# Layer-norm statistics shared between VectorE and ScalarE, and one group of small matmuls moved, in a two-layer spectral and MLP kernel

## The chip, the cores and the metric

The kernel runs on one core of one Trainium2 chip. The metric is the device time of one execution in microseconds (us), median of several. Every time below comes from runs that were classed as undisturbed ("fast"). One profile is one execution.

## The reference, cut to what matters

```python
x = A_x                                              # 2048 x 1024, bf16
x = x + A(layernorm(x), w_r, w_i)                    # 2D FFT, filter, inverse FFT
x = x + B(layernorm(x), w1, b1, w2)                  # mish MLP, 1024 -> 3584 -> 1024
x = x + A(layernorm(x), w_r, w_i)
x = x + B(layernorm(x), w1, b1, w2)

def layernorm(x, eps=1e-5):
    m = jnp.mean(x, axis=-1, keepdims=True)
    v = jnp.var(x, axis=-1, keepdims=True)
    return (x - m) / jnp.sqrt(v + eps)
```

The change touches the very first layernorm, over sixteen tiles of 128 rows, and the point where each A hands over to its B.

## The kernel before

The first layernorm is not applied to x. Its scales 1/std are multiplied into the table of the first FFT stage ("scaled"), so the first matmul has to wait for the scales of all sixteen tiles. The statistics are made by two engines, each taking whole tiles:

```python
def first_scales(self):
    for j in range(10):
        self.stats_dve(j)              # VectorE: two bn_stats of 512, one bn_aggr
    for j in range(10, 16):
        self.stats_act(j)              # ScalarE: Copy and Square, each with accum_out
    self.sums_to_mv(10, 6)             # the combining step, VectorE
    self.root(0, 16)                   # sqrt on ScalarE, reciprocal on VectorE
    ...                                # transpose the scales: RT (SBUF) and a copy in PSUM

def scaled(self, j):                   # table of column group j times the scales
    if j == 3: ...                     # ScalarE, 8 small ones
    prog = self.pool if j in (1, 4, 6, 8, 10, 12, 14, 15) else self.dve
    self.op(prog, lambda e: e.tensor_tensor(self.MN.ap[:, n, :], ..., ALU.mult), ...)
```

GpSimd (`pool`) has a second duty before that. It issues twelve of the loads of x in its second layout, and holds them back until the last tile of the first layout has landed:

```python
for q in range(4):
    for h in range(8):
        prog = self.pool if q and h % 2 else sp
        self.dma(prog, self.XR.ap[h:P:8, 32 * q:32 * q + 32, :], ...,
                 reads=[self.r_xs[15]] if prog is self.pool else [])
```

At the start of layer B, `rest(bank)` is a group of fifteen matmuls of 96 columns that finishes a piece of A, and copies the result out on ScalarE. `transposed` transposes a normalised tile on TensorE and copies it out on VectorE. `mm1` is the first MLP matmul:

```python
self.root(0, 2)
rest(0)
for j in range(2):
    xn[j] = self.apply(j)
for j in range(2):
    transposed(0, j, xn[j])
self.warm(ACT.Mish)                    # loads the Mish table
rest(3)
...
for fg in range(4):
    mm1(0, fg, 0, ...)
    rest(3)
```

## Time and profile before

| | us |
|---|---|
| time, median of the first three runs | 1014.7 (1014.44 to 1017.05) |
| statistics: combining step starts | 20.12 |
| scales ready | 22.52 |
| GpSimd's table scalings start | 23.28 |
| first matmul of the second FFT stage (L719) | 40.07 |
| layer B of layer 0: first small group (L1014, 96 columns) | 119.89 |
| first large matmul (L1103) | 124.12 |

The numbers (but for the first row) are starts in the profiled execution, counted from the start of the span; for the scales it is the end of the copy that brings them in place. Each row is a place where one engine waits for another. The profile names instructions by source line; the changed kernel has seven lines more, so its line numbers are up to 7 higher, and its L441 is the new sum where L441 before is ScalarE's pass.

### The profile page before, as it was taken

What the parts mean: (1) busy time and instruction counts of PE and PEld (TensorE: products, weight loads), DVE (VectorE), ACT (ScalarE), POOL (GpSimd) and SP (SyncE); (2) the same over time, 40 slices, a digit from 0 to 9 for tenths busy, and PEclk for the clock granted to TensorE, in tenths of its full rate; (3) what the DMA queues carried; (4) which work ended last, traced back from release to release, by engine and by line L of the source; (5) the groups of instructions that cost most, each with busy time, mean ns of one, the idle gap of its engine ahead of it and who ended that gap; (6) DMA issues with size and microseconds to landing.
All of it is one profiled execution on the core that took longest, in us unless ns stands there. A gap on an engine that the chain in (4) does not pass through costs nothing.

```text
span 1013.4 us, 13752 instructions
## 1 busy us (share of the span) xinstructions
PE 958.2 (95%) x5826; PEld 506.4 (50%) x5826; DVE 326.5 (32%) x679; ACT 347.7 (34%) x487; POOL 81.5 (8%) x114
## 2 busy tenths in 40 slices
PE   0799799999999999999999979999999999999998
PEld 0667575444444444444456748644444444444443
DVE  6797568002444000033347736830011100000111
ACT  7798474440000443300029837534100023430000
POOL 3831000000000000002421100000000000000000
PEclk9999899999999999999999998999999999999999
DMA  9969823652111220002922875246411212100000
GB/s 281 281 191 321 213 60 115 198 196 65 48 46 32 74 82 21 1 21 85 199 60 84 232 187 154 77 161 203 129 25 45 73 52 83 43 1 11 21 27 26
DMA packets 154205, 107.00 MB, mean 106 GB/s; under 512 B 74448, under 2 KB 133664, under 8 KB 154144
## 3 DMA queue, kind: packets, MB, share of 16 engines
q1 hardware_dynamic: 143056, 78.61, 27.5%
q0 software_dynamic: 8912, 25.84, 8.7%
q10 hardware_dynamic: 2176, 1.66, 0.5%
q8 instruction: 47, 0.77, 0.3%
q14 instruction: 14, 0.11, 0.0%
HBM read 80.85 MB, written 20.71 MB: 100 GB/s over the span
## 4 chain that ended last, share of the span: by engine, by line
PE 87%; DVE 5%; DMA 4%; ACT 2%; POOL 1%; issue 0%; SPq 0%; ACTq 0%; POOLq 0%; DVEq 0%
PE PS L1121 38%; PE PS L1103 38%; PE PS L793 2%; PE PS L719 2%; PE PS L1014 2%; PE PS L818 2%; DMA XS<-in_A_x_dram 1%; DMA ARENA<-c_bt 1%; POOL ARENA L249 1%; PE PS L1069 1%; DMA ARENA<-u_scratch 1%; DVE ARENA L637 1%; DMA u_scratch<-ARENA 1%; DVE ARENA L775 1%; DVE ARENA L610 1%; ACT ARENA L635 1%
## 5 line engine op out<-in xcount | busy, mean ns | idle before, releaser
L1103 PE MATMUL PS<-ARENA 128*128 128x512 bf16 (+1 forms) x1984 | 390.9, 358 | 0.2
L1121 PE MATMUL PS<-ARENA 128*128 128x512 bf16 x1792 | 387.4, 379 | 0.0
L1107 ACT ACTIVATE ARENA<-PS,B 128x512 bf16<-128x512 f32 (+1 forms) x248 | 159.4, 645 | 411.6 <-PE PS L1103 411.0
L1103 PEld LDWEIGHTS PS<-ARENA 128*128 128x128 bf16 x1984 | 193.0, 98 | 192.7 <-DVE ARENA L1074 0.9
L1121 PEld LDWEIGHTS PS<-ARENA 128*128 128x128 bf16 x1792 | 175.4, 98 | 211.4
L1132 DVE TENSOR_TENSOR XS<-PS,XS 128x512 bf16<-128x512 f32 x63 | 43.6, 692 | 582.3 <-PE PS L1121 582.3
L460 DVE BATCH_NORM_STATS2 BN<-XS 128x6 f32<-128x512 bf16 x99 | 63.8, 673 | 6.1 <-DMA XS<-in_A_x_dram 5.1
L249 POOL DMA_DIRECT2D xn_scratch<-ARENA x12 | 6.5, 541 | 373.4 <-DVE ARENA L512 373.4
L793 PE MATMUL PS<-ARENA 128*128 128x256 bf16 x256 | 32.4, 273 | 3.9 <-DVE ARENA L782 3.2
L771 ACT ACTIVATE ARENA<-PS 128x1024 bf16<-128x1024 f32 x32 | 33.3, 1071 | 4.5 <-PE PS L767 4.5
L432 ACT ACTIVATE RS<-MV,EPS 128x2 f32<-128x2 f32 (+2 forms) x5 | 1.5, 297 | 96.6 <-DVE MV L463 84.4
L719 PE MATMUL PS<-FD,ARENA 128*128 128x256 bf16 (+1 forms) x256 | 31.8, 271 | 2.4 <-ACT ARENA L635 1.2
L1014 PE MATMUL PS<-MT,ARENA 128*128 128x32 bf16 (+1 forms) x512 | 22.3, 201 | 9.7 <-DMA ARENA<-u_scratch 6.3
L804 ACT ACTIVATE ARENA<-PS 128x1024 bf16<-128x1024 f32 x28 | 29.8, 1087 | 3.9 <-PE PS L793 3.9
L793 PEld LDWEIGHTS PS<-ARENA 128*128 128x128 bf16 x256 | 24.0, 98 | 12.0 <-DVE ARENA L782 5.7
L568 ACT ACTIVATE ARENA<-PS 128x1440 bf16<-128x1440 f32 (+1 forms) x22 | 25.5, 1160 | 10.8 <-PE PS L793 3.9
L775 DVE TENSOR_TENSOR ARENA<-ARENA 128x1024 bf16<-128x1024 bf16 x32 | 22.0, 688 | 19.8 <-ACT ARENA L771 19.8
L719 PEld LDWEIGHTS PS<-FD,ARENA 128*128 128x128 bf16 x256 | 24.4, 98 | 6.5 <-DVE ARENA L637 1.4
L1014 PEld LDWEIGHTS PS<-MT,ARENA 128*128 128x128 bf16 x512 | 20.6, 104 | 12.7 <-issue 7.2
L818 PE MATMUL PS<-ARENA,BD 128*128 128x256 bf16 x192 | 24.9, 273 | 1.6 <-DVE ARENA L572 1.6
L862 ACT ACTIVATE ARENA<-PS 128x1024 bf16<-128x1024 f32 x24 | 25.3, 1090 | 0.0
L512 DVE TENSOR_SCALAR ARENA<-XS,MV,RS 128x1024 bf16<-128x1024 bf16 x47 | 24.3, 543 | 0.9
(85 smaller groups left out, 530.6 us busy)
## 6 DMA issues: line engine op xcount, KB each, us to landing
ARENA<-in_B_w_dram SPq DMA_DIRECT2D x56, 512.0 KB, 3.9
ARENA<-in_B_w_dram SPq DMA_DIRECT2D x56, 256.0 KB, 4.3
u_scratch<-ARENA SPq DMA_DIRECT2D x14, 512.0 KB, 3.8
ARENA<-u_scratch SPq DMA_DIRECT2D x14, 512.0 KB, 6.1
w_scratch<-ARENA POOLq DMA_DIRECT2D x8, 512.0 KB, 6.9
ARENA<-w_scratch POOLq DMA_DIRECT2D x8, 512.0 KB, 5.3
out_dram<-XS SPq DMA_DIRECT2D x16, 256.0 KB, 2.1
ARENA<-xn_scratch POOLq DMA_DIRECT2D x15, 256.0 KB, 9.1
```

Of the source, the lines that this page charges most:

```text
L460: self.op(self.dve, lambda e: e.bn_stats(self.BN[:, j, 6 * h:6 * h + 6], self.XS[:, j, 512 * h:512 * h + 512]), reads=[self.r_xs[j]], part ...
L719: fns.append(lambda e: e.matmul(dst, at(r), FD[:, t:t + n], start=start, stop=stop))
L771: self.op(act, lambda e: e.activation(x.ap.rearrange("p a b -> p (a b)"), ps, ACT.Copy, scale=SIG), reads=banks, writes=[x.res])
L775: self.op(dve, lambda e: e.tensor_tensor(ta.ap, x.ap, wt.ap[:, 0:1, :].to_broadcast([P, 2, 512]), ALU.mult), reads=[x.res, wt.res], writes ...
L793: fns.append(lambda e, c=c, part=part: e.matmul(ps[:, c * 256:(c + 1) * 256], yk.ap[:, part, c * P:(c + 1) * P], t[:, (128, 0)[part]:(384, ...
L804: self.op(act, lambda e: e.activation(v.ap[:, :, i, :], src, ACT.Copy), reads=banks, parts=[v.res])
L818: fns.append(lambda e, dst=dst, part=part, c=c: e.matmul(dst, BD[:, c:c + P], mov(kd, part), start=(part == 0), stop=(part == 1)))
L1014: fns.append(lambda e, l=l: e.matmul(self.PS[:, bank + l // k, l % k * w:(l % k + 1) * w], self.UT.ap[:, u0 + l, :], self.MT[:, 8 * lo:8 * ...
L1103: fns.append(lambda e, db=db, bank=bank, fl=fl: e.matmul(PS[:, bank, 0:w], wb.ap[:, db, fl * P:(fl + 1) * P], x.ap[:, db, tok], start=(db ...
L1107: self.op(act, lambda e, bank=bank, ft=ft: e.activation(at.ap[:, ft, tok], PS[:, bank, 0:w], ACT.Mish, bias=self.B1[:, ft:ft + 1]), reads= ...
L1121: fns.append(lambda e, i=i, ft=ft: e.matmul(PS[:, bank, :], at.ap[:, ft, t * P:(t + 1) * P], W2[ft].ap[:, h * 512:(h + 1) * 512], start=(i ...
L1132: self.op(dve, lambda e: e.tensor_tensor(xs, PS[:, bank, :], xs, ALU.add), reads=[self.r_bank[bank]], writes=[self.r_xs[j]])
```

## The change

The intent is to shorten the opening. Nine tiles are shared: VectorE makes the sum with a scalar operation that accumulates, ScalarE the sum of squares. Seven tiles stay with VectorE alone. The input is loaded in an order meant to suit this. In both layers B the second `rest` group moves in front of the transposes.

```diff
-        for a, b in ((10, 11), (0, 1), (1, 3), (11, 12), (3, 6), (12, 14), (6, 10), (14, 16)):
+        for a, b in ((7, 8), (0, 1), (8, 9), (1, 2), (9, 11), (2, 4), (11, 13), (4, 7), (13, 16)):
...
+    def stats_act(self, j, summed=False):
+        if summed:
+            self.op(self.dve, lambda e: e.tensor_scalar(self.junk2.ap, x, 1.0, 0.0, op0=ALU.mult, op1=ALU.add, accum_out=sums[:, 0:1]),
+                    reads=[self.r_xs[j]], writes=[self.junk2.res], parts=[rs])
         for i, f in enumerate((ACT.Copy, ACT.Square)):
+            if summed and i == 0:
+                continue
...
-        for j in range(10):
+        for j in range(7):
             self.stats_dve(j)
-        for j in range(10, 16):
-            self.stats_act(j)
-        self.sums_to_mv(10, 6)
+            self.stats_act(7 + j, True)
+        for j in (14, 15):
+            self.stats_act(j, True)
+        self.sums_to_mv(7, 9)
...
         rest(0)
+        rest(3)
         for j in range(2):
             xn[j] = self.apply(j)
         for j in range(2):
             transposed(0, j, xn[j])
         self.warm(ACT.Mish)
-        rest(3)
```

More of the change, by code (lines that the diff above doesn't have):

```diff
@@ L363, in layout @@
         self.o = dict(XR=0, Z=0, X=12 * K, T=20 * K, YK=28 * K, V=40 * K, JT=48 * K, M0=49 * K, IDF=49 * K + 256, RT=50 * K,
-                      JUNK=51 * K, WR=54 * K, YS=96 * K, UT=64 * K, MN=64 * K, Y=96 * K, XN=128 * K, U=128 * K,
+                      JUNK=51 * K, JUNK2=62 * K, WR=54 * K, YS=96 * K, UT=64 * K, MN=64 * K, Y=96 * K, XN=128 * K, U=128 * K,
                       FT=140 * K, BT=144 * K + 512, WT=self.W1_OFF)
@@ L377, in prologue @@
         xt = self.x[0].rearrange("(t p) d -> p t d", p=P)
-        for a, b in ((10, 11), (0, 1), (1, 3), (11, 12), (3, 6), (12, 14), (6, 10), (14, 16)):
-            self.dma(self.act if a == 10 else sp, self.XS[:, a:b, :], xt[:, a:b, :], f"x{a}", writes=self.r_xs[a:b])
+        for a, b in ((7, 8), (0, 1), (8, 9), (1, 2), (9, 11), (2, 4), (11, 13), (4, 7), (13, 16)):
+            self.dma(self.act if a == 7 else sp, self.XS[:, a:b, :], xt[:, a:b, :], f"x{a}", writes=self.r_xs[a:b])
         self.warm(ACT.Sqrt)
@@ L434, in root @@
         self.op(self.dve, lambda e: e.reciprocal(r, a), writes=rr)
-    def stats_act(self, j):
+    def stats_act(self, j, summed=False):
         act = self.act
@@ L578, in first_scales @@
         dve, act = self.dve, self.act
-        for j in range(10):
+        self.junk2 = self.alloc("JUNK2", self.o["JUNK2"], [self.D])
+        for j in range(7):
             self.stats_dve(j)
-        for j in range(10, 16):
-            self.stats_act(j)
-        self.sums_to_mv(10, 6)
+            self.stats_act(7 + j, True)
+        for j in (14, 15):
+            self.stats_act(j, True)
+        self.sums_to_mv(7, 9)
         self.root(0, 16)
```

## The prediction

> **What bounds the kernel now.** I read the page first, then the chain of waits up to 130 us, then the order of time of each engine in the first 45 us and around 118 to 130 us and 608 to 623 us, where the two parts of the change lie.
>
> The page says that TensorE is the bound over the whole span:
>
> ```profile
> PE 958.2 (95%) x5826; PEld 506.4 (50%) x5826; DVE 326.5 (32%) x679; ACT 347.7 (34%) x487; POOL 81.5 (8%) x114
> PE   0799799999999999999999979999999999999998
> ```
>
> TensorE's busy row has a 0 only in the first slice (25 us) and short dips elsewhere. Nothing in the opening overlaps with the long matmul stages, so a microsecond gained or lost before the first matmul is one of the total, unless a later wait swallows it. The opening in three engines' order of time (start, duration, engine, line, operation, count, idle before it):
>
> ```profile
> 5.85 0.21 DVE L463 BATCH_NORM_AGGREGATE MV<-BN 128x2 f32<-128x12 f32 x1
> 5.98 1.23 DVE L460 BATCH_NORM_STATS2 BN<-XS 128x6 f32<-128x512 bf16 x2
> 7.25 0.21 DVE L463 BATCH_NORM_AGGREGATE MV<-BN 128x2 f32<-128x12 f32 x1
> ...
> 4.70 1.06 ACT L441 ACTIVATE ARENA<-XS 128x1024 bf16<-128x1024 bf16 x1 [2.02 <-DMA XS<-in_A_x_dram]
> 5.66 0.19 ACT L441 ACTIVATION_READ_ACCUMULATOR ARENA<-XS 128x1 f32 x1
> 5.88 1.06 ACT L441 ACTIVATE ARENA<-XS 128x1024 bf16<-128x1024 bf16 x1
> ...
> 20.12 0.17 DVE L452 TENSOR_SCALAR MV<-BN 128x12 f32<-128x12 f32 x1 [0.86 <-ACT ARENA L441]
> ...
> 22.23 0.29 DVE L591 COPY ARENA<-PS 128x128 f32<-128x128 f32 x1 [0.64 <-PE PS L589]
> ...
> 15.56 7.62 POOL L249 DMA_DIRECT2D ARENA<-in_A_x_dram  x12 [14.70 <-DMA XS<-in_A_x_dram]
> 23.28 14.87 POOL L610 TENSOR_TENSOR ARENA<-ARENA 128x1024 bf16<-128x1024 bf16 x8
> ```
>
> Three things are to be seen. One tile of statistics on VectorE (two BATCH_NORM_STATS2 and one aggregate) has a period of 7.37 - 5.98 = 1.39 us. One ACTIVATE with its accumulator read has a period of 5.88 - 4.70 = 1.18 us, so one tile on ScalarE (sum and square) costs 2.36. Both engines finish almost together: VectorE's tenth tile ends at 19.26, ScalarE's sixth at 20.09, and the combining step starts at 20.12. The scales are in place at 22.52 (22.23 + 0.29). And GpSimd is a second limit close behind: it issues twelve transfers from the landing of the last input tile until 23.18, and only then starts its eight table scalings, 14.87 us in one run, of which the last feeds the last matmul of the first stage. So **earlier** statistics could hardly gain, because GpSimd would not start before 23.28; **later** ones cost all but 23.28 - 22.57 = 0.7 us, after which GpSimd would wait for the scales.
>
> The second place, the start of layer B (layer 0 shown; layer 1 at 608 to 623 us looks the same):
>
> ```profile
> 119.89 1.38 PE L1014 MATMUL PS<-MT,ARENA 128*128 128x96 bf16 x15 [1.67 <-ACT XS L568]
> 121.45 1.89 PE L1069 MATMUL PS<-IDENT,ARENA 128*128 128x128 bf16 x16 [0.17 <-DVE ARENA L512]
> 123.13 0.97 PE L1014 MATMUL PS<-MT,ARENA 128*128 128x96 bf16 x15
> 124.12 1.92 PE L1103 MATMUL PS<-ARENA 128*128 128x256 bf16 x16
> ...
> 123.37 0.69 DVE L1074 COPY ARENA<-PS 128x1024 bf16<-128x1024 bf16 x1 [0.16 <-PE PS L1069]
> ```
>
> And from the view of stretches (TensorE, weight loads, VectorE, ScalarE, GpSimd, then the granted clock):
>
> ```profile
> 122.00:123.00 1.00, 1.00 (x12) 1.00 (x10) 0.48 (x1) 0.98 (x2) 0.00 (x0) 0.50 1.19 302
> ```
>
> The second group of fifteen small matmuls (L1014) runs while VectorE copies the transposes out of PSUM (until 124.06), and the large matmuls (L1103) start right behind that copy: the group is hidden there. Before the transposes TensorE waits only 0.17 us. From 122 to 123 us the granted clock (the number after GpSimd's) is 0.50; the same view has 0.77 for 123 to 124 and 1.00 after that.
>
> **What the Trainium skill says.** "VectorE: DVE Perf Modes", section "The perf-mode tier table", gives bf16 `tensor_scalar` in SBUF four elements a cycle; whoever reads only that expects about 0.3 to 0.5 us for a 1024-element sum. But "SBUF — State Buffer", section "Who interferes with whom", lists among the operations of the two-port modes "`tensor_scalar` (not the form that also writes out its accumulator)", and "PSUM — Partial Sum Buffer", section "Specifications (TRN2)", names `tensor_scalar` as sending two elements at a time only without an accumulator output, and gives 1.04 ns per element otherwise. Together: one element a cycle for the form that the change uses. The trace before has no such instruction and can neither confirm nor deny it; it has one-element-a-cycle work of 1024 elements (L610, 1212 ns each, 1.13 us apart), which shows what that pace costs. "TensorE: Matmul & The Clock Gate", section "What's actually happening", has a half-rate clock after an idle window of about 3.4 us and full rate after a busy one; the granted clock of 0.50 above, after a wait for a transfer, agrees.
>
> **Part one, the statistics.** Removed from VectorE: three of ten tiles, 3 x 1.39 = 4.17 us. Added to VectorE: nine sums of 1024 elements. I take the main instruction at 1.09 us (1024 elements at the pace of the 512-element BATCH_NORM_STATS2, two of which take 1.23 us at a mean of 0.673, so 0.56 apart) and the accumulator read at 0.11, by analogy with ScalarE's, which adds 0.12. That is 1.2 us a sum, an estimate, 10.8 in all. ScalarE's share shrinks from 12 passes to 9, 10.6 us; fed by the input, whose last part lands near 15.3 as before, it ends around 19. So VectorE becomes the bound of the opening: before it ended at 19.26, with 0.53 us of waiting for input that its slower pace removes: 19.26 - 0.53 - 4.17 + 10.8 = 25.36, or 25.4. The combining step starts there in place of 20.12: 5.3 us later. GpSimd has 0.7 of slack, so its scalings, and with them the first stage's end, move by 4.6 us. Starting earlier relative to the rest, the loads that are already under way (filters, tables) will be in place sooner; TensorE's waits for transfers between 40 and 106 us are only 0.71 and 0.36 us, so I credit 0.2. The rest of that stretch is TensorE 61.6 us busy of 65.9 and moves as a block. Net: **+4.4 us**.
>
> **Part two, the fifteen matmuls in front of the transposes**, in both layers. They would start when the first group has issued, near 121.1 (15 matmuls of 96 columns at half clock, 80 ns apart, the pace of 1.2 us between 119.89 and there). At half clock they take another 1.2, so the transposes start near 122.3 in place of 121.45, 0.85 later; a part comes back as the clock rises near 123.5 whatever is run. The large matmuls then start near 124.7 in place of 124.12: +0.6 in layer 0, and near 615.9 in place of 615.16: +0.75 in layer 1, where the clock rises later. What is gained is on ScalarE: the group's result is copied out before the table load and not behind it, so the first Mish waits for TensorE and no longer for the copy, and banks come free sooner. TensorE waits for such a bank once, 0.29 us at 128.43 in layer 0; that I take off. Net: 0.3 + 0.7 = **+1.0 us**.
>
> Sum: 1014.7 + 4.4 + 1.0 = 1020.1; I put down 1020.0.
>
> **The rivals.** *The sum is fast* (two or four elements a cycle, 0.45 to 0.7 us): VectorE ends at 18.6 to 20.9, the combining step moves by -1.5 to +0.8. GpSimd starts at 23.28 either way, so the gain is about nothing: 1014.5 to 1016, with part two. For it: the split of 7 and 9 balances the engines only with a sum of about 0.5 us, so the author must have expected it. Against it: the two sentences of the skill. I give it one in ten. *The sum is at one element but the delay is absorbed*, because the tables' transfers were the true limit after 40 us: then +2 or so, 1017 to 1018. Against it: TensorE's waits for transfers there sum to about one microsecond. *Part two gains*, because ScalarE is the limit between 121 and 134 us (its idle gaps there are 0.16 to 0.4 us): then -0.5 a layer, and the total is near 1018. Against it: TensorE has no gap either, and the transposes stand behind the moved group. *The accumulating form is slower still* (a drain before its accumulator read, 1.4 us in all): two microseconds more, 1022.
>
> **Range and chances.** Executions of the kernel before spread from 1014.44 to 1017.05, medians less. The slow-sum family spans 1017 to 1022.5, the fast one lies at 1014.5 to 1016. Predicted 1020.0, range 1016.8 to 1022.5. Two per cent are 20 us; neither part can move that much: faster 0.01, same 0.98, slower 0.01.
>
> **What would show it.** In the profile of the changed kernel: the accumulating TENSOR_SCALAR at 1.05 to 1.25 us each with a small read behind it (0.3 to 0.6 would refute step one); the combining step at about 25.4 with VectorE busy up to it and ScalarE done near 19; GpSimd's scalings starting at about 27.9, held by the scales and no longer by its transfers; the first layer's TensorE work displaced by 4 to 5 us up to 118 us. At layer B: thirty small matmuls in a row, transposes some 0.85 us later relative to the first group, a gap of TensorE before the first L1103. The prediction is wrong if the sums are fast, if the displacement shrinks well below 4 us between 40 and 110 us, or if the distance from the first L1014 group to the large matmuls does not grow.

## The result, and the profile after

The changed kernel took 1020.16 us, median of 4 runs (1019.21 to 1022.61), against 1014.78 (1014.44 to 1017.05, 4 runs). The ratio is 1.0052, with a 95% interval of 1.0029 to 1.0075. A ratio is the mean time of one kernel's fast runs over that of the other's of the same rounds, so it is not quite the ratio of the medians. By the 2% rule this is "same"; clear of noise it is half a per cent slower. The page of the changed kernel, engines and TensorE's busy row:

```profile
PE 952.7 (94%) x5742; PEld 506.7 (50%) x5826; DVE 333.0 (33%) x688; ACT 344.3 (34%) x481; POOL 81.8 (8%) x114
PE   0699699999999999999998978999999999999998
```

Nothing large moved: VectorE is 6.5 us busier, ScalarE 3.4 less. TensorE's shorter busy time is no saving, because 84 matmul records are missing from this trace (5742 of 5826, while the weight loads are complete). The place is found in the opening, in order of time. First VectorE (start, duration, operation, count; a bracket at the end of a line holds the idle time of the engine just before, and what ended it):

```profile
5.83 0.21 DVE L468 BATCH_NORM_AGGREGATE MV<-BN 128x2 f32<-128x12 f32 x1
5.96 1.17 DVE L441 TENSOR_SCALAR_CACHE_REDUCE ARENA<-XS 128x1024 bf16<-128x1024 bf16 x1
7.05 0.08 DVE L441 DVE_READ_ACCUMULATOR ARENA<-XS 128x1 f32 x1
7.05 1.28 DVE L465 BATCH_NORM_STATS2 BN<-XS 128x6 f32<-128x512 bf16 x2
...
22.25 0.08 DVE L441 DVE_READ_ACCUMULATOR ARENA<-XS 128x1 f32 x1
22.37 1.22 DVE L441 TENSOR_SCALAR_CACHE_REDUCE ARENA<-XS 128x1024 bf16<-128x1024 bf16 x1
23.51 0.08 DVE L441 DVE_READ_ACCUMULATOR ARENA<-XS 128x1 f32 x1
23.63 1.22 DVE L441 TENSOR_SCALAR_CACHE_REDUCE ARENA<-XS 128x1024 bf16<-128x1024 bf16 x1
24.77 0.08 DVE L441 DVE_READ_ACCUMULATOR ARENA<-XS 128x1 f32 x1
24.89 0.17 DVE L457 TENSOR_SCALAR MV<-BN 128x18 f32<-128x18 f32 x1
...
27.00 0.29 DVE L598 COPY ARENA<-PS 128x128 f32<-128x128 f32 x1 [0.64 <-PE PS L596]
```

The accumulating operation appears under a name of its own and takes 1.17 us; its read of the accumulator takes 0.08. From a sum to the statistics behind it is 7.05 - 5.96 = 1.09 us; where another sum follows it is 23.63 - 22.37 = 1.26. Once its first tile has landed, VectorE goes on without a pause until the combining step at 24.89. ScalarE's and GpSimd's rows:

```profile
18.01 0.19 ACT L446 ACTIVATION_READ_ACCUMULATOR ARENA<-XS 128x1 f32 x1
25.50 0.31 ACT L432 ACTIVATE RS<-MV,EPS 128x16 f32<-128x16 f32 x1 [7.30 <-DVE MV L459]
```

```profile
14.96 7.64 POOL L249 DMA_DIRECT2D ARENA<-in_A_x_dram  x12 [14.10 <-DMA XS<-in_A_x_dram]
27.37 14.88 POOL L617 TENSOR_TENSOR ARENA<-ARENA 128x1024 bf16<-128x1024 bf16 x8 [4.77 <-DVE ARENA L598]
```

ScalarE is done at 18.20 and then idles for 7.30 us. GpSimd, done with its issues at 22.60, idles for 4.77 us until the scales are there. So what was a balance of two engines with GpSimd close behind has become one engine's work.

TensorE at the start of layer B in layer 0, and the granted clock from the view of stretches (in each line the number after GpSimd's):

```profile
124.02 2.58 PE L1021 MATMUL PS<-MT,ARENA 128*128 128x96 bf16 x30 [1.67 <-ACT XS L573]
126.40 1.91 PE L1076 MATMUL PS<-IDENT,ARENA 128*128 128x128 bf16 x16
129.10 1.92 PE L1110 MATMUL PS<-ARENA 128*128 128x256 bf16 x16 [0.79 <-DVE ARENA L1081]
130.85 0.80 PE L1021 MATMUL PS<-MT,ARENA 128*128 128x96 bf16 x15
```

```profile
127.00:128.00 1.00, 1.00 (x13) 1.00 (x10) 0.51 (x1) 1.00 (x1) 0.00 (x0) 0.50 1.19 290
128.00:129.00 1.00, 0.31 (x3) 0.04 (x1) 0.84 (x3) 0.98 (x2) 0.00 (x0) 0.66 1.19 297
```

Thirty small matmuls now stand in one row, the transposes follow 2.38 us after the first of them (1.56 before), and TensorE has a gap of 0.79 us in front of the large matmuls, in which VectorE copies the transposes out. Over the whole trace the delay builds up like this:

| start of | before | after | difference |
|---|---|---|---|
| combining step | 20.12 | 24.89 | 4.77 |
| GpSimd's scalings | 23.28 | 27.37 | 4.09 |
| second FFT stage | 40.07 | 44.16 | 4.09 |
| first small group, layer 0 | 119.89 | 124.02 | 4.13 |
| first large matmul, layer 0 | 124.12 | 129.10 | 4.98 |
| first small group, layer 1 | 610.87 | 615.92 | 5.05 |
| first large matmul, layer 1 | 615.16 | 620.26 | 5.10 |
| end of the span | 1013.4 | 1018.5 | 5.1 |

Between these two traces the statistics cost 4.1 us and nothing swallows it. In layer 0 the moved group costs 0.85 more, in layer 1 only 0.05.

### The profile page after: what moved, and what is told of

It reads as the page before. It is cut to its first block, busy times and chain, and to the rows that moved or that the text cites. A ratio compares the mean times of both kernels' runs of the same rounds, so it can differ in the third digit from the quotient of the medians.

```text
span 1018.5 us, 13674 instructions
## 1 busy us (share of the span) xinstructions
PE 952.7 (94%) x5742; PEld 506.7 (50%) x5826; DVE 333.0 (33%) x688; ACT 344.3 (34%) x481; POOL 81.8 (8%) x114
## 4 chain that ended last, share of the span: by engine, by line
PE 86%; DVE 7%; DMA 3%; ACT 2%; issue 1%; POOL 0%; SPq 0%; ACTq 0%; DVEq 0%
PE PS L1128 38%; PE PS L1110 38%; PE PS L800 2%; PE PS L1021 2%; PE PS L726 2%; PE PS L825 2%; DMA ARENA<-c_bt 1%; DVE ARENA L441 1%; DMA ARENA<-u_scratch 1%; DVE BN L465 1%; PE PS L1076 1%; DVE ARENA L644 1%; DMA u_scratch<-ARENA 1%; DVE ARENA L617 1%; DVE ARENA L782 1%
## 5 line engine op out<-in xcount | busy, mean ns | idle before, releaser
L465 DVE BATCH_NORM_STATS2 BN<-XS 128x6 f32<-128x512 bf16 x93 | 60.3, 677 | 5.6 <-DMA XS<-in_A_x_dram 4.5
## 6 DMA issues: line engine op xcount, KB each, us to landing
ARENA<-xn_scratch POOLq DMA_DIRECT2D x15, 256.0 KB, 10.8
```

Of the source, the lines that this page charges most:

```text
L465: self.op(self.dve, lambda e: e.bn_stats(self.BN[:, j, 6 * h:6 * h + 6], self.XS[:, j, 512 * h:512 * h + 512]), reads=[self.r_xs[j]], part ...
```

## The experiments

Ten kernels were run. All ten came back as correct by the comparison with the reference, even the three whose sums are wrong: presumably the means are near zero, so that a wrong one in nine tiles stays within the tolerance; nothing shows it.

The theory: part one costs about 4 us, because a sum with an accumulator runs at one element a cycle, and GpSimd's transfer issues hide the first 0.7 us of it. Part two costs up to 0.9 us a layer, by the granted clock. The rivals are named with each run.

**Part one alone** (`part_one`): the group at layer B is put back.

```diff
         rest(0)
-        rest(3)
...
         self.warm(ACT.Mish)
+        rest(3)
```

> Only the statistics part of the change; layer B as before. Theory (the two parts add, and the sums cost one element a cycle): GpSimd's scalings start at 27.4 as in the changed kernel, 4.1 us later than before, nothing of it is swallowed: 1014.7 + 4.1 = 1018.8 us (1018.3 to 1019.4). Rival (part two is what costs, the opening is absorbed by transfers): within 1 us of the kernel before. Rival (part two gains on its own and hides some of part one): slower than the changed kernel, over 1020.5.

Measured: 1019.29 us (6 runs, 1018.54 to 1021.58) against 1015.67 (11 runs); ratio 1.0034, interval 1.0016 to 1.0053. In its trace GpSimd's scalings start at 27.41 and the second stage at 44.20, 4.13 us after the kernel before. The median is inside the range given, though the kernel before stood 1.0 us higher in this call than in the one on which the range was built, so that is partly luck; the ratio's interval (about 1.6 to 5.4 us) holds the 4.1, and the rival of an absorbed opening falls by the trace: the first small group of layer 0 is at 124.17, 4.28 late. The new order of loading was not run alone; in the changed kernel VectorE waits for no input after its first tile, so that order can't be what holds it.

**Part two alone** (`part_two`): the kernel before, with the group moved.

```diff
         rest(0)
+        rest(3)
...
         self.warm(ACT.Mish)
-        rest(3)
```

> Only the fifteen matmuls put ahead of the transposes, in both layers; the statistics as before. Theory: the transposes start later by what the fifteen cost, 1.2 us at half clock and 0.65 at full, and the first large matmul by 0.1 to 0.85 per layer depending on the clock granted there: +0.2 to +1.7 in all, most likely +0.9, 1015.6 us. The gap between the first small matmul and the first large one, 4.23 us (layer 0) and 4.29 us (layer 1) in the kernel before, grows to about 5.1 where the clock is 0.50 throughout. Rival (earlier freeing of banks and an earlier table load pay): -0.5 to -1.0, 1013.9 us.

Measured: 1016.50 us (6 runs, 1013.82 to 1019.10) against 1015.67; ratio 1.0002, interval 0.9981 to 1.0024. The times cannot tell +1 from -1. In the trace the first large matmul comes 4.82 us after the first small group in both layers. That is more than the kernel before (4.23 and 4.29), but less than the 5.1 expected for a half-rate clock throughout (in layer 0 the clock had risen by 123.0). The question is taken up again below, over all traces.

**A cheap sum** (`short_sum`): part one, with a sum over 256 of the 1024 elements; wrong.

```diff
-  e.tensor_scalar(self.junk2.ap, x, 1.0, 0.0, ..., accum_out=sums[:, 0:1])
+  e.tensor_scalar(self.junk2.ap[:, 0:256], x[:, 0:256], 1.0, 0.0, ..., accum_out=sums[:, 0:1])
```

> Part one only, and each accumulating sum reads 256 elements in place of 1024. The result is wrong on purpose (the mean of nine tiles is taken from a quarter of them). At one element a cycle 256 elements cost what 1024 would at four a cycle, so this shows what the change would have been worth with a fast sum. Theory one element a cycle: each main instruction near 0.37 us in place of 1.17. Theory GpSimd is the second limit: VectorE ends near 18, the combining step starts near 18.3, the scales are there near 20.7, but GpSimd's scalings start only when its transfers are issued, near 22.6, so the time is 1014.7 - 0.6 = 1014.1 (1013.6 to 1014.8). Rival (the statistics alone set the opening): the whole 1.8 us is gained, 1012.9.

Measured: 1016.36 us (6 runs) against 1015.67; ratio 1.0004, interval 0.9984 to 1.0023. The groups of VectorE in the changed kernel and in this one (count, busy us, mean ns):

```profile
L441 DVE TENSOR_SCALAR_CACHE_REDUCE ARENA<-XS 128x1024 bf16<-128x1024 bf16 x9 | 10.6, 1178 | 0.1
L441 DVE DVE_READ_ACCUMULATOR ARENA<-XS 128x1 f32 x9 | 0.8, 83 | 0.0
```

```profile
L441 DVE TENSOR_SCALAR_CACHE_REDUCE ARENA<-XS 128x256 bf16<-128x256 bf16 x9 | 3.4, 378 | 0.1
```

The slope is (1178 - 378) / 768 = 1.04 ns per element, one element a cycle at the 0.96 GHz that "VectorE: DVE Perf Modes", section "Specifications", gives. With the sum cheap the combining step starts at 18.81 and the scales are ready at 21.20, both earlier than in the kernel before. The time does not follow, and GpSimd's rows say why:

```profile
14.70 7.68 POOL L249 DMA_DIRECT2D ARENA<-in_A_x_dram  x12 [13.84 <-DMA XS<-in_A_x_dram]
22.48 14.88 POOL L617 TENSOR_TENSOR ARENA<-ARENA 128x1024 bf16<-128x1024 bf16 x8
```

GpSimd issues transfers until 22.38 and starts its scalings at once, with no idle time in front: the scales have been waiting for it for 1.3 us. The second stage starts at 39.27, 0.80 earlier than in the kernel before, but GpSimd's first issue came 0.86 earlier (14.70 against 15.56), because the last input landed earlier in this execution. So even a sum at four elements a cycle would have brought next to nothing, as the first rival of the prediction had it. The run's own rival, 1.8 us gained, lies just outside the interval (1.6 us gained at most).

**A plain scalar operation** (`plain_scalar`): part one, with the accumulator output taken off the 1024-element operation and a tiny accumulating one put behind it; wrong.

```diff
-  e.tensor_scalar(self.junk2.ap, x, 1.0, 0.0, ..., accum_out=sums[:, 0:1])
+  e.tensor_scalar(self.junk2.ap, x, 1.0, 0.0, op0=ALU.mult, op1=ALU.add)
+  e.tensor_scalar(self.junk3.ap[:, 0:8], x[:, 0:8], 1.0, 0.0, ..., accum_out=sums[:, 0:1])
```

> Part one only, with each sum done as a plain tensor_scalar over the same 1024 elements with no accumulator output, followed by an accumulating one over 8 elements. The result is wrong on purpose. Theory (it is the accumulator output that takes the fast mode away): the plain form takes 0.30 to 0.45 us against 1.17, the small one about 0.15; VectorE ends near 19 and the time is within 0.7 us of the kernel before. Rival (a 1024-element tensor_scalar of this kind is slow anyway, or the cost is the read of the accumulator): 0.9 us or more each, and about 1018 to 1019. Side question: if the fast form takes the memory ports that GpSimd needs, GpSimd's twelve transfer issues take longer than 7.64 us.

Measured: 1016.44 us (6 runs) against 1015.67; ratio 0.9999, interval 0.9979 to 1.0019. Its groups:

```profile
L441 DVE TENSOR_SCALAR ARENA<-XS 128x1024 bf16<-128x1024 bf16 x9 | 3.7, 407 | 0.0
L443 DVE TENSOR_SCALAR_CACHE_REDUCE ARENA<-XS 128x8 bf16<-128x8 bf16 x9 | 1.4, 151 | 0.0
```

The same 1024 elements through the same operation take 0.407 us without an accumulator output and 1.178 with it; seven of the nine plain ones took 0.37. The read of the accumulator is 0.08 us in either kernel and no part of the difference. So it is the accumulator output that costs the speed, and the rival of a slow scalar operation falls. The side question stays half open: GpSimd's twelve issues took 7.86 us in place of 7.64, and the last two plain operations, inside the issues, took 0.44 and 0.61, but one inside the issues took 0.37. About 0.05 of the excess has another cause that can be seen: sums with no other statistics between them are that much longer in other kernels too (1.22 against 1.17 in the changed kernel). The scales were ready at 22.15, earlier than in the kernel before, yet the second stage started only at 41.14: the last input landed late here, GpSimd issued from 16.40 to 24.26, and its scalings waited for that.

**GpSimd relieved** (`late_xr`): the kernel before, with four of the twelve issues given to ScalarE behind its square root.

```diff
+                if q == 3 and h % 2:
+                    continue
                 prog = self.pool if q and h % 2 else sp
...
         self.root(0, 16)
+        for h in (1, 3, 5, 7):
+            self.dma(act, self.XR.ap[h:P:8, 96:128, :], xv[h][:, 96:128, :], "xr3ACT", parts=[self.r_xr[3]])
```

> The kernel before, with the last four of GpSimd's twelve transfer issues taken over by ScalarE, which issues them while it waits after its square root. Theory (GpSimd's issues, 7.6 us from the landing of the last input tile, are what holds its scalings in the kernel before): eight issues take 5.1 us, GpSimd starts its scalings when the scales are there, near 22.6 in place of 23.28, and the first stage ends 0.7 us earlier: 0.5 to 0.9 us less than the kernel before of the same rounds. Rival (the scales hold it): no change in the start of the scalings.

Measured: 1015.18 us (5 runs) against 1015.62 (11 runs); ratio 0.9995, interval 0.9983 to 1.0007: by the times, nothing certain. GpSimd's rows:

```profile
14.71 5.16 POOL L249 DMA_DIRECT2D ARENA<-in_A_x_dram  x8 [13.86 <-DMA XS<-in_A_x_dram]
22.22 14.87 POOL L615 TENSOR_TENSOR ARENA<-ARENA 128x1024 bf16<-128x1024 bf16 x8 [2.34 <-DVE ARENA L596]
```

Now GpSimd idles 2.34 us for the scales and starts 0.09 us after they are ready (22.13): the gate is gone, as the theory had it. In this execution the last input tile had landed early (GpSimd's first issue, which follows it, is at 14.71, against 15.56 in the kernel before), so even twelve issues would have ended near 22.4 and the relief was worth only 0.2 us. Over the twelve traces that first issue lies between 14.46 and 16.40 us; by the same working, a start at 15.56 would make the relief worth the 0.7, an estimate that no run shows.

**A cheap sum and GpSimd relieved** (`short_sum_late_xr`): both edits; wrong.

> The cheap-sum kernel (256 elements a sum, wrong result on purpose) with the same relief of GpSimd. In the cheap-sum kernel the scales were there near 21.2 and GpSimd began at 22.48. Theory (GpSimd's gate swallowed the rest of what a cheap sum gains): with the gate gone GpSimd starts near 21.3 and the first matmul of the second stage comes near 38.1 (39.27 in the cheap-sum kernel, 40.07 before). Rival (something else limits the stage): the start moves and the end stays near 39.3.

Measured: 1014.35 us (5 runs) against 1015.62; ratio 0.9989, interval 0.9975 to 1.0002: by the times, again nothing certain. The combining step came at 19.34 (VectorE waited longer for an input and went on at 9.63, against 9.10 in `short_sum`), the scales at 21.80, GpSimd's start at 21.88 and the second stage at 38.67. The start was 0.5 us later than expected and the end with it, and the rival, an end that stays near 39.3, falls. Over the traces the stage has a plain rule. In eleven of twelve the second stage starts 16.78 or 16.79 us after GpSimd's scalings (40.07 - 23.28 before, 44.16 - 27.37 after, 39.27 - 22.48 with cheap sums, 38.67 - 21.88 here); in `late_xr_spin_two` it is 17.03. GpSimd starts within 0.1 us of the later of two things, the scales and the end of its issues.

**More idle matmuls ahead of layer B** (`spin_before`): to see whether the half-rate clock there can be avoided. `spin` issues matmuls whose result nobody uses.

```diff
-        self.spin(4, 0)
+        self.spin(10 if li == 0 else 18, 0)
```

> The kernel before, with 10 (layer 0) and 18 (layer 1) idle matmuls of 512 columns in place of 4, run while TensorE waits for the transfers ahead of layer B; they end before the data land. Theory (the half-rate clock there comes from the idle wait): the granted clock between the first small matmul group and the first large one is above 0.50 for more of that stretch, and the distance from the first small group to the one behind the first large matmuls, 5.99 and 6.04 us in the kernel before, falls by up to 0.6. Rival (the clock falls because the 32-column matmuls leave the array too idle): the clock and the distances stay as before.

Measured: 1014.75 us (6 runs) against 1015.62; ratio 0.9992, interval 0.9978 to 1.0005. In layer 0 the clock was full through the whole stretch, and the distance from the first small group to the one behind the first large matmuls was 5.32 us; in layer 1 it was 5.99, with a clock of 0.75 from 611 to 615 us. That looked like a success of the idle matmuls, until the next runs. It need not have: in the same trace the clock is 0.50 in each microsecond from 115 to 118, just ahead of the first small group at 119.08. The half-rate time was not avoided; it fell earlier.

**The same with the group moved** (`spin_part_two`):

> Part two with the same idle matmuls. Where the clock is full the fifteen matmuls cost 0.65 us and not 1.2: theory: the distance from the first small group to the one behind the first large matmuls exceeds that of the kernel with the old order and idle matmuls by 0.1 to 0.6 us a layer (0.24 us a layer is the difference of the means of the profiles so far: 6.52 against 6.28). Rival (the new order is free at full clock): no difference or less.

Measured: 1016.43 us (6 runs) against 1015.62; ratio 1.0004, interval 0.9991 to 1.0017. The distances were 6.37 and 6.42 us, and in layer 0 the clock was 0.50 from 116 to 120 us in spite of the idle matmuls.

**Both helpers together, without and with the moved group** (`late_xr_spin`, `late_xr_spin_two`):

> The kernel before with both helpers: four of GpSimd's issues on ScalarE, and more idle matmuls ahead of layer B. If they add: 0.7 us from the opening (scalings start with the scales) and 0 to 1.3 us from a fuller clock at the two starts of layer B, so 0.7 to 2 us below the kernel before of the same rounds. If the clock is a matter of chance and not of the idle matmuls, only the 0.7.

> The same with part two of the change on top. The distance from the first small matmul group to the one behind the first large matmuls was 5.99 to 6.95 us in the old order (mean 6.33 of 12 without extra idle matmuls) and 6.10 to 6.83 in the new (mean 6.52 of 4). If the new order costs about 0.2 us a layer: 6.4 to 6.7 here where the clock is half, and a time within 1 us of the kernel without it. If it costs the 0.5 a layer of the prediction: 1 us slower than that kernel.

Measured: 1014.88 us (6 runs) and 1015.22 us (5 runs) against 1015.44 (11 runs); ratios 0.9996 (0.9981 to 1.0011) and 0.9994 (0.9980 to 1.0007). Neither is faster than the kernel before beyond doubt. The distances were 7.04 and 5.89 us without the moved group, 6.75 and 6.12 with it. The 7.04 is the longest of all traces, in a kernel with the extra idle matmuls. Against the same stretch in layer 0 of `spin_before`, by the view of stretches (`spin_before` first, the clock after GpSimd's number):

```profile
119.08:124.40 5.32, 4.28 (x63) 3.81 (x63) 4.96 (x12) 5.08 (x7) 0.00 (x0) 1.00 1.19 296
```

```profile
119.28:126.32 7.04, 6.86 (x62) 6.07 (x63) 6.03 (x15) 5.42 (x7) 0.00 (x0) 0.56 1.18 305
```

The same instructions take 5.32 us at a full clock and 7.04 at 0.56. The idle matmuls do not secure the full clock, so their expected gain is not shown, and neither is the 0.7 from the opening. In one-microsecond stretches, all twelve traces show the clock at 0.50 for some time around both starts of layer B, with or without the idle matmuls. Worked out from the mean clock of these stretches, it lasted about 3.4 us (`spin_before`, 114.7 to 118.1), 6.8 (`part_two`, 116.2 to 123.0) or 10.2 (`late_xr`, 114.4 to 124.7). What differs between executions is how long it lasts and where it falls. That fits the rival named with `spin_before`, the 32-column matmuls, which run in all of them; no run tested it alone.

**The moved group over all traces.** The distance from the first group of 96-column matmuls to the group behind the first sixteen large ones holds all work that part two reorders:

| order | kernel | layer 0 | layer 1 |
|---|---|---|---|
| old | before | 5.99 | 6.04 |
| old | part_one | 6.17 | 6.42 |
| old | short_sum | 6.25 | 6.39 |
| old | plain_scalar | 6.48 | 6.49 |
| old | late_xr | 6.95 | 6.47 |
| old | short_sum_late_xr | 5.99 | 6.27 |
| old | spin_before | 5.32 | 5.99 |
| old | late_xr_spin | 7.04 | 5.89 |
| new | changed kernel | 6.83 | 6.10 |
| new | part_two | 6.58 | 6.58 |
| new | spin_part_two | 6.37 | 6.42 |
| new | late_xr_spin_two | 6.75 | 6.12 |

The old order's mean is 6.26 us (16 values), the new order's 6.47 (8 values): 0.2 us a layer, with spreads of 5.32 to 7.04 and 6.10 to 6.83. The new order is probably a little slower, but its cost is not settled against that spread; it is not a gain of the 0.5 us a layer that one rival had. Nor is anything won back behind this stretch: from the first small group of layer 0 to that of layer 1 it is 491.1 us in the mean of the old order (490.02 to 492.24, 8 traces) and 491.5 in the new (491.24 to 491.90, 4 traces). What is shown is that the trace of the kernel before, with 5.99 and 6.04, was at the lucky end of its own order.

## Why the prediction was right or wrong, point by point

- **Total.** 1020.0 was put down with a range of 1016.8 to 1022.5; the median is 1020.16. Part one makes up most of it, by the right mechanism. That the number fits to 0.2 us is luck: in the traces compared, part one cost 4.1 us (4.4 predicted) and part two 1.0 (as predicted), but part two's 1.0 came as 0.9 in layer 0 and next to nothing in layer 1, and over all traces it is about 0.4.
- **The sum costs one element a cycle.** Right, shown by the slope and by the plain form. The estimate of 1.2 us a sum was 0.1 too high for six of the nine: the next operation starts together with the read of the accumulator (at 7.05), so these take 1.09 us. The last three, with another sum or the combining step behind them, take 1.21 to 1.26; there the analogy with ScalarE's read holds. In all it is 10.3 us in place of 10.8, and the combining step came at 24.89 and not at 25.4.
- **ScalarE done near 19, GpSimd held by the scales.** Right: 18.20, and an idle time of 4.77 us that ends with the scales.
- **GpSimd has 0.7 us of slack.** Right in mechanism: 4.77 us late at the combining step became 4.09 at GpSimd's start. The predicted 4.6 was too large by the excess of the sums. (The 22.57 in its working is in none of the lines shown; it is the 22.52 at which the scales are in place and a few hundredths until GpSimd can start, 0.08 in the changed kernel.) What it left out is that the slack depends on when the last input lands. In the four traces with the opening of the kernel before, GpSimd's scalings start at 23.28, 23.18, 22.57 and 22.18, which is 0.76, 0.90, 0.19 and 0.09 us after the scales. With part one they start at 27.37 and 27.41. So part one costs 4.1 to 5.2 us, depending on the execution that it is compared with.
- **A credit of 0.2 us for loads that are in place earlier.** Wrong: the delay is 4.09 at the second stage and 4.13 at layer B. Nothing is swallowed on the way: from the second stage to the first small group of layer 0 it is 79.6 to 80.0 us in eleven of the twelve traces, early or late (80.8 in `spin_part_two`).
- **Part two, layer 0: +0.6, less 0.29 for a bank wait.** The transposes came 0.82 us later (0.85 predicted) and the first large matmul 0.85. The 0.29 did not come back, because it never was on the path: it stands on the weight-load row at 128.43, while TensorE's own row shows no idle time there, and that group follows the large matmuls at the same 1.92 us in both kernels (126.51 to 128.43, 131.49 to 133.41). The step "TensorE waits for such a bank once" misread a row.
- **The half-rate clock.** The prediction says that the 0.50 after a wait for a transfer agrees with the idle window of about 3.4 us that it cites. The trace doesn't show that in layer 0: between 112 and 119.9 us TensorE waited 1.62, 0.83 and 1.67 us, and never for 3.4 at once. In layer 1 there was a wait of 3.83 us, and there it can agree.
- **Part two, layer 1: +0.75.** It was 0.05 in this trace: the clock was still full for about the first 0.9 us of the thirty small matmuls, and they took 1.65 us and not 2.38. In the old order the transposes start 1.55 or 1.56 us after the first small group in all 16 places, whatever the clock, because they wait for the normalised tile (0.17 or 0.18 us at a half clock, up to 0.75 at a full one). The moved group fills that wait. So at a half clock it delays the transposes by 0.82 us (2.38, in six places of the new order), and at a partly full one by 0.1 (1.65 and 1.67, in two). The prediction knew only the wait of 0.17. The failed step is "a part comes back as the clock rises near 123.5 whatever is run". It took the moment of the rise in one execution for a property of the kernel. In the trace before, the clock rose just in time for the large matmuls in both layers; in most other traces of the same order it did not, and the new order, which puts the large matmuls later, loses less by a late rise (its first sixteen large matmuls take 1.92 us in all 8 places, those of the old order 1.91 to 2.77). Over all traces part two costs about 0.2 us a layer and not 0.5, and even the sign isn't certain.
- **The rival "the sum is fast".** Its time, "about nothing" gained, is what the two kernels with cheap sums took. The bet of the change would not have paid even if its premise had held, for GpSimd's reason that the prediction gave.

## What to carry to other kernels

Before work is moved to another engine, take the price of the exact form of the instruction from a run: the operation that ran 1024 elements in 0.37 us took 1.17 once it had to give out an accumulator. When two engines are balanced, look for the third that stands just behind them (here GpSimd, which is still issuing transfers), since it decides what an improvement is worth, while a loss beyond its slack is paid in full; and read that slack from several executions, for here it was 0.1 to 0.9 us. And where a stretch runs at a clock that changes with time, compare many executions of it before putting a number on a reordering.

## What the Trainium skill lacked or had wrong

- "VectorE: DVE Perf Modes", section "The perf-mode tier table", gives bf16 `tensor_scalar` in SBUF the fourfold mode with no exception for the form with an accumulator output. The runs show 1178 ns against 407 ns (370 undisturbed) for 1024 elements, and 1.04 ns per element. The exception is mentioned on two other pages only, which the prediction quotes, and there they are right.
- The same page, section "Two Vector instructions with no wait between them", says that an operation with an accumulator output is two instructions, but gives no cost for the second: it is 83 ns here. A statistics operation behind it starts in the same moment (7.05 and 7.05), another sum 0.12 us later (22.25 and 22.37).
- "TensorE: Matmul & The Clock Gate", section "Why this matters for your kernels", asks for no gaps of TensorE over about 3 us. In layer 0 of `late_xr_spin` the waits between 112 and 119.3 us were 0.30, 0.91 and 1.67 us, with 32-column matmuls in between, and the clock fell to 0.50 all the same, for 119 to 125 us. The page gives no figure for how dense narrow matmuls must be to hold the clock.
- No page was found that says for how long GpSimd itself is held by issuing a transfer such as these: twelve took 7.64 us in the changed kernel, 0.64 each, and in the kernel before it is what its scalings wait for.
